# Turning tiles on TensorE instead of in the DMA queue, in a two-layer attention and MLP kernel

## The chip, the cores and the metric

The kernel runs on one core of one Trainium2 chip. The metric is device time in microseconds (us). Before the change it is 1536.79 us, the median of three runs (1535.73 to 1537.83).

## What is computed

Two layers of attention and a feed-forward block each, over one sequence of 2048 tokens of width 512, with 32 heads of 16 columns. Weights are the same in both layers.

```python
def _A_ref(x, wqkv, wo):
    qkv = (x @ wqkv).reshape(B, S, 3, H, Dh)          # H = 32, Dh = 16
    q, k, v = ...
    p = _softmax(jnp.einsum("bhqd,bhkd->bhqk", q, k) * Dh ** -0.5)
    o = jnp.einsum("bhqk,bhkd->bhqd", p, v)
    return o.reshape(B, S, D) @ wo

def _B_ref(x, w1, b1, w2, b2):
    h = _gelu(_layernorm(x) @ w1 + b1)                # F = 1376
    return h @ w2 + b2

x = x + _A_ref(_layernorm(x), wqkv, wo)
x = x + _B_ref(_layernorm(x), w1, b1, w2, b2)
x = x + _A_ref(_layernorm(x), wqkv, wo)
x = x + _B_ref(_layernorm(x), w1, b1, w2, b2)
```

The attention is the bulk of it: 2 layers x 32 heads x 2048 x 2048 exponentials.

## The kernel before

**Attention.** Four heads make a head group (hg, eight of them); each head has 32 rows of a 128-row tile, 16 of data, one for a bound on the score and the rest zero pads. KT holds the keys turned, 128 rows by 2048 tokens per head group; QT holds the queries of up to 512 tokens turned and scaled. A score tile is one key block of 128 tokens times 512 queries of one head: one matmul that uses 32 rows of the array (L1536) and fills one PSUM bank. There are 4096 such banks of scores. Most get their exponential on ACT (ScalarE), three or two banks at a time in turn (banks 0 to 2 and 3 to 4, L1521), into the tile PT. The tiles of five key blocks in 16 (DK) can go to DVE (VectorE) in place of ACT: L1628 loads the bank as a 16-bit pattern that approximates the exponential (dp), and L1659, L1667, L1614 and L1615 make three copies of it with shifted bits, whose values are multiplied with copies of V scaled to match (vs). So a bank on DVE needs four PV matmuls (L1741), a bank on ACT one. PV adds up in a bank of its own (ACCB); at the end of a segment (one layer, query chunk and head group) L1771 transposes it out, and L1807 writes the normalised result into ob.

**The rest.** job_qkv_tile and job_first_tile make queries, keys and values of a tile of 128 tokens; job_post and job_ffn make the output projection and the feed-forward block; job_tail does so for the last tile. Between them tiles must be turned by 128x128 blocks: the normalised input (xn to xnT, L993, and to yT, L1872), the attention output (ob to OT, ot_dma, L1816), keys (qk to KT, L1004 and L1136), and queries. The queries lie unturned in device memory (q_scr) and flow_q turns them as it loads them (L1248). In layer 3 (the name of the second layer) the keys of the first twelve tiles wait in k_scr until KT is free, and job_kload turns them on the way back (L1301). All these are DMA transposes, issued by SP. A few tiles are turned by TensorE and copied out of PSUM: the first four (L1112, copied by ACT, L1113), tiles 4 to 7 of the keys of layer 1 (TPE, L989, copied by DVE, L990), the first queries of two head groups (L1204) and the last tile (L2053).

**What sets the order.** No order is written by hand. Sched holds tasks with a priority, the resources that they read and write, and a duration that the author put in; it runs a model of the engines and lays every task on its engine's stream when it would be next. Scores come first, PV next, and the rest fills in. PSUM banks that are not scores' belong to the pool mb. After the first part of layer 1, take_d sends a bank of scores to DVE whenever DVE has time and one of two banks is free: DLANE (5) or MISCB (7), the last one of the pool. Every four groups of scores the planner's thresholds are set by the next character of a hint string (Hint.ORDER). When the plan is complete, refill goes over PE's stream once more and puts matmuls on a zero tile (zw, L1425, L1427, L1429) into gaps; their results are not used.

Of the kernel before, what the change touches and what calls it, by code (L numbers as in the profile page):

```python
# [14 lines left out]
ALU = mybir.AluOpType  # L15
# [263 lines left out]
class Sched:  # L279
# [168 lines left out]
    def run(self):  # L448
        while True:
# [20 lines left out]
            if t.mate is not None:  # L470
                lim = max(pick[0], self.P.free["dve"]) + self.LOOK["dve"]
                both = next((o for o in self.pend["dve"] if o.mate is not None and o.mate[0] == t.mate[0] and (o.mate[1] < t.mate[1]) == (o.mate[2] < t.mate[2]) and self.task_ready(o) <= lim), None)
# [41 lines left out]
ACCB = 6  # L514
MISCB = 7
DTAIL = 8
DURGE = 8
# [8 lines left out]
TPE = range(4, 8)  # L526
# [14 lines left out]
class Hint:  # L541
# [3 lines left out]
    ORDER = '617843148821304205503107024723209000040207043042340397211914350542770442973009430070000450240024504940493349800001430000505010133104559a211a25403202330431702000300020315024491400100220000100700000140303000510323100000881337000000003040223443052000002459894171985995005343441000044430740448998b224440804240010009a541'  # L545
# [13 lines left out]
class Builder:  # L559
# [45 lines left out]
    def alloc(self, es):  # L605
# [67 lines left out]
        self.q_scr = nc.dram_tensor("q_scr", [2, S, 1024], BF16, kind="Internal").ap()  # L673
        self.k_scr = nc.dram_tensor("k_scr", [S, 1024], BF16, kind="Internal").ap()
# [6 lines left out]
        pl["mb"] = Pool([7, 5, 4, 3, 2, 1, 0])  # L681
# [294 lines left out]
    def job_qkv_tile(self, L, tt, slot, i, left, prio, what):  # L976
# [10 lines left out]
        if L == 1 and what == "kv" and tt in TPE:  # L987
            b = yield ("get", "mb")
            yield Task("pe", prio, [I(lambda e, k=k, b=b: e.transpose(self.psbf(b)[:, k * 128:(k + 1) * 128], xnr[:, k * 128:(k + 1) * 128], self.ident[:, :]), [RX, ("ident",)], [("ps", b)], 0.06, [("ps", b)]) for k in range(4)])  # L989
            yield Task("dve", prio, [I(lambda e, b=b: e.tensor_copy(out=xnT, in_=self.psbf(b)[:, 0:512].rearrange("p (c t) -> p c t", c=4)), [("ps", b)], [RXT], 0.4)])  # L990
            S_.release("mb", b)
        else:
            yield self.dma(lambda e: e.dma_start_transpose(xnT, xnr), [RX], [RXT], prio, 1.31, 1.2)  # L993
# [8 lines left out]
        def kstore():  # L1002
            if direct:
                yield self.dma(lambda e: e.dma_start_transpose(self.KT[:, :, tt * 128:(tt + 1) * 128], self.qks(qs)[:, 1, :]), [QK], [("kt", hg, tt) for hg in range(8)], prio, 1.31, 1.9)  # L1004
            else:
                yield self.dma(lambda e: e.dma_start(self.k_scr[tt * 128:(tt + 1) * 128, :], self.qks(qs)[:, 1, :]), [QK], [("kscr", tt)], prio, 0.38, (1.65, 1.05))
            S_.mark(("ks", L, tt))
# [11 lines left out]
        if "k" in what:  # L1019
# [4 lines left out]
            S_.spawn(kstore(), prio)  # L1024
# [32 lines left out]
        yield Task(eng, prio, [I(lambda e: e.tensor_tensor(out=sq, in0=v4, in1=v4, op=ALU.mult), [("qk", qs, k) for k in range(k0, k1)], SR, 0.14 + 0.00845 * N if eng == "dve" else 1.04)])  # L1057
        if "k" in what:
            yield Task("dve", prio, [self.norms(self.n2k[:, tt, :], ("n2k", tt), ss, 1)])
            S_.mark(("n2k", L, tt))  # L1060
# [8 lines left out]
        if "q" in what:  # L1069
            li = L // 2  # L1070
            yield self.dma(lambda e: e.dma_start(self.q_scr[li, tt * 128:(tt + 1) * 128, :], self.qks(qs)[:, 0, :]), [QQ], [("qscr", L, tt)], prio, 0.38, (1.65, 1.05))
# [30 lines left out]
    def job_first_tile(self, tt, slot, i, left, prio):  # L1102
# [32 lines left out]
        def store():  # L1135
            yield self.dma(lambda e: e.dma_start_transpose(self.KT[:, :, tt * 128:(tt + 1) * 128], self.qks(qs)[:, 1, :]), [QK], [("kt", hg, tt) for hg in range(8)], prio, 1.31, 1.9)  # L1136
            S_.mark(("ks", 1, tt))
# [1029 lines left out]
```

## Time and profile before

| What | Value |
|---|---|
| median of the runs | 1536.79 us |
| the profiled execution | 1537.7 us, its span 1535.9 us |
| granted TensorE clock | 1.00 in all but one of 40 slices |
| matmuls on the zero tile | 2247, 354 us of PE's busy time |
| DMA transposes | 229 |
| bytes moved by DMA | 90.55 MB, DMA engines busy 25.6% of the span |

The profile is of one execution. A row of a group gives the line, the engine, what is written from what, shapes, the count, then busy time in us and the mean of one in ns, and the idle time of the engine just before them with what ended it. Durations of one engine's instructions can overlap, so a busy time can be less than count times mean. In the waits an engine and line stand first, then what they waited for, the total in us, how often and the longest.

### The profile page before, as it was taken

What the parts mean: (1) busy time and instruction counts of PE and PEld (TensorE: products, weight loads), DVE (VectorE), ACT (ScalarE), POOL (GpSimd) and SP (SyncE); (2) the same over time, 40 slices, a digit from 0 to 9 for tenths busy, and PEclk for the clock granted to TensorE, in tenths of its full rate; (3) what the DMA queues carried; (4) which work ended last, traced back from release to release, by engine and by line L of the source; (5) the groups of instructions that cost most, each with busy time, mean ns of one, the idle gap of its engine ahead of it and who ended that gap; (6) DMA issues with size and microseconds to landing.
All of it is one profiled execution on the core that took longest, in us unless ns stands there. A gap on an engine that the chain in (4) does not pass through costs nothing.

```text
span 1535.9 us, 41170 instructions
## 1 busy us (share of the span) xinstructions
PE 1486.8 (97%) x17654; PEld 491.3 (32%) x17654; DVE 1442.2 (94%) x2661; ACT 1502.5 (98%) x1346; POOL 343.0 (22%) x570
## 2 busy tenths in 40 slices
PE   9999999999999999999999999999999999999998
PEld 3222222222222222222322332222222222344555
DVE  8799999999999999999999899999999989998786
ACT  8999999999999999999999999999999999999897
POOL 3576321102120022202322138220002000020110
PEclk9999999999999999999999999999999999999999
DMA  6663102213312123214842332210011001120221
GB/s 163 120 154 91 32 22 34 51 35 68 82 48 63 37 64 84 56 35 100 138 69 64 60 87 63 53 30 18 22 36 35 14 27 32 36 49 18 73 67 30
DMA packets 212487, 90.55 MB, mean 59 GB/s; under 512 B 182251, under 2 KB 207184, under 8 KB 212304
## 3 DMA queue, kind: packets, MB, share of 16 engines
q1 hardware_dynamic: 212304, 87.92, 25.6%
q8 instruction: 138, 2.26, 0.6%
q14 instruction: 45, 0.37, 0.1%
HBM read 36.81 MB, written 19.48 MB: 37 GB/s over the span
## 4 chain that ended last, share of the span: by engine, by line
ACT 44%; PE 27%; DVE 24%; issue 3%; POOL 2%; DMA 0%; DVEq 0%; POOLq 0%
ACT PT L1521 41%; DVE dp L1628 10%; PE ps L1536 9%; PE ps L1741 8%; PE ps L1943 3%; DVE dp L1667 3%; PE ps L1882 2%; PE ps L1016 2%; ACT h L1934 2%; DVE dp L1615 2%; DVE dp L1659 1%; PE ps L1425 1%; DVE accT L1771 1%; DVE st L933 1%; DVE dp L1614 1%
## 5 line engine op out<-in xcount | busy, mean ns | idle before, releaser
L1521 ACT ACTIVATE PT<-ps 128x1536 bf16<-128x1536 f32 (+1 forms) x1256 | 1422.0, 1309 | 20.6 <-PE ps L1536 18.8
L1628 DVE TENSOR_SCALAR dp<-ps 128x512 uint16<-128x512 f32 x979 | 648.8, 679 | 33.7 <-PE ps L1536 30.4
L1536 PE MATMUL ps<-QT,KT 32*128 32x512 bf16 (+2 forms) x5120 | 602.6, 340 | 23.9 <-ACT PT L1521 7.5
L1741 PE MATMUL ps<-PT,V 128*17 128x512 bf16 (+2 forms) x3899 | 491.1, 338 | 0.6 <-issue 0.5
L1741 PE MATMUL ps<-dp,vs 128*17 128x512 bf16 (+2 forms) x3663 | 460.8, 339 | 2.7 <-issue 1.8
L1536 PEld LDWEIGHTS ps<-QT,KT 32*128 32x128 bf16 x5120 | 174.1, 91 | 543.6 <-ACT PT L1521 297.6
L1262 POOL TENSOR_SCALAR QT<-qraw,scl,qbias 128x512 bf16<-128x512 bf16 (+2 forms) x91 | 75.2, 827 | 762.8 <-PE ps L1536 754.3
L1741 PE MATMUL ps<-dp,V 128*17 128x512 bf16 (+2 forms) x1221 | 232.3, 340 | 1.6 <-DVE accT L1771 1.2
L1667 DVE TENSOR_SCALAR dp<-dp 128x2048 uint16<-128x2048 uint16 x310 | 214.3, 694 | 4.9 <-PE ps L1741 1.8
L1741 PEld LDWEIGHTS ps<-dp,vs 128*17 128x17 bf16 x3663 | 124.1, 89 | 114.1 <-issue 84.8
L1741 PEld LDWEIGHTS ps<-PT,V 128*17 128x17 bf16 x3899 | 126.9, 89 | 94.2 <-issue 75.1
L1429 PE MATMUL ps<-zw 128*32 128x448 bf16 (+23 forms) x1514 | 147.1, 322 | 0.1
L1659 DVE TENSOR_SCALAR dp<-dp 128x1024 uint16<-128x1024 uint16 (+1 forms) x298 | 126.1, 426 | 2.6
L1427 PE MATMUL ps<-zw 32*128 32x444 bf16 (+7 forms) x386 | 119.5, 332 | 0.0
L1615 DVE TENSOR_SCALAR dp<-dp 128x4096 uint16<-128x4096 uint16 x91 | 111.0, 1225 | 0.6 <-PE ps L1741 0.4
L1882 PE MATMUL ps<-yT,wf 128*128 128x512 bf16 (+5 forms) x440 | 102.7, 340 | 2.1 <-issue 1.0
L1016 PE MATMUL ps<-wqkv,xnT 128*128 128x512 bf16 x336 | 91.7, 382 | 4.1 <-DVE h L1029 1.1
L1425 PE MATMUL ps<-zw 128*128 128x448 bf16 (+14 forms) x347 | 87.4, 338 | 4.4 <-DVE onec L809 2.1
L1287 POOL TENSOR_SCALAR vs<-V 128x340 bf16<-128x340 bf16 (+2 forms) x72 | 64.3, 894 | 23.0 <-PE ps L1741 16.2
L1741 PEld LDWEIGHTS ps<-dp,V 128*17 128x17 bf16 x1221 | 58.2, 89 | 34.6 <-issue 19.4
L1614 DVE TENSOR_SCALAR dp<-dp 128x2048 uint16<-128x2048 uint16 x97 | 67.8, 700 | 0.0
L1771 DVE STREAM_TRANSPOSE accT<-ps 128x512 f32<-128x512 f32 (+2 forms) x96 | 59.2, 617 | 5.3 <-PE ps L1741 5.0
(201 smaller groups left out, 1053.4 us busy)
## 6 DMA issues: line engine op xcount, KB each, us to landing
vs<-vs_scr SPq DMA_DIRECT2D x64, 255.0 KB, 2.8
wf<-in_B_w_dram SPq DMA_DIRECT2D x90, 128.0 KB, 2.5
q_scr<-qk SPq DMA_DIRECT2D x20, 256.0 KB, 2.0
k_scr<-qk SPq DMA_DIRECT2D x12, 256.0 KB, 2.1
out_dram<-xres SPq DMA_DIRECT2D x16, 128.0 KB, 1.7
vs_scr<-vs SPq DMA_DIRECT2D x8, 255.0 KB, 3.3
xres<-in_A_x_dram SPq DMA_DIRECT2D x7, 256.0 KB, 5.3
v_scr<-vst SPq DMA_DIRECT2D x12, 136.0 KB, 1.7
```

Source lines behind the costliest of these rows:

```text
L1016: yield Task("pe", prio if c0 == 0 else min(prio, HINT.LIN2), [I(lambda e, c=c: e.matmul(self.ps[:, b, :], lhsT=xnT[:, c, :], rhs=self.wqk ...
L1425: fn = lambda e: e.matmul(self.ps[:, b, 0:w], lhsT=self.zw[:, 0:128], rhs=self.zw[:, 0:w], start=st, stop=st, skip_group_check=True)
L1427: fn = lambda e: e.matmul(self.ps[:, b, 0:w], lhsT=self.zw[32 * p:32 * p + 32, 0:128], rhs=self.zw[32 * p:32 * p + 32, 0:w], start=st, sto ...
L1429: fn = lambda e: e.matmul(self.ps[32 * p:32 * p + 32, b, 0:w], lhsT=self.zw[:, 0:32], rhs=self.zw[:, 0:w], start=st, stop=st, skip_group_c ...
L1521: S_.submit(Task("act", 1e-5 * gi, [I(lambda e, pt=pt, n=n, b0=b0: e.activation(out=self.PT[:, pt:pt + n, :], in_=self.ps[:, b0:b0 + n, :] ...
L1536: return [I(lambda e, kb=kb, i=i: e.matmul(self.ps[:, b, i * W:(i + 1) * W], lhsT=self.KT[32 * hp:32 * hp + 32, hg, kb * 128:(kb + 1) * 12 ...
L1615: return lambda e: e.tensor_scalar(out=self.both(x[1], y[1]), in0=self.both(x[0], y[0]), scalar1=float(SHIFT[2]), scalar2=None, op0=ALU.add)
L1628: self.S_.submit(Task("dve", 0.0, [I(lambda e: e.tensor_scalar(out=self.dpu(u)[:, w * 512:(w + 1) * 512], in0=self.ps[:, b, :], scalar1=BI ...
L1659: t = Task("dve", prio(), [I(lambda e: e.tensor_scalar(out=self.dpu(u + 1)[:, 0:N], in0=self.dpu(u)[:, 0:N], scalar1=float(SHIFT[1]), scal ...
L1667: t = Task("dve", prio(), [I(lambda e: e.tensor_scalar(out=self.dpp(v)[:, :, 0:N], in0=self.dpp(u)[:, :, 0:N], scalar1=float(SHIFT[2]), sc ...
L1741: ops.append((nth[j, sh] + 0.1 * i, I(lambda e, hp=hp, v=v, ap=ap[:, i * W:(i + 1) * W], first=first and i == 0, W=W: e.matmul(self.ps[32 ...
L1882: yield Task("pe", self.soft(pr if c0 == 0 else min(pr, HINT.LIN2)) if y0 == 0 else pr, [I(lambda e, c=c: e.matmul(self.ps[0:M, b, 0:W], l ...
```

## The change

Every tile that a DMA transpose turned is now turned by TensorE into a bank of the pool mb (turn, and ot_turn for the attention output) and copied out of it by DVE, in layer 1 from key tile 8 on by ACT. Queries and the stored keys of layer 3 are turned in place, in their qk buffer, before they are stored: q_scr and k_scr hold them turned, and the loads of qraw and KT are plain copies. The turned tile lies over the pads of the qk buffer, so repad clears them again on POOL. The roles of banks 6 and 7 are exchanged, so that DLANE (5) and MISCB (6) are neighbours, and two loads by DVE that are ready together, one from each, become one instruction (d_join, kind 0). DLANE leaves the common pool only when all keys of layer 1 are stored. take_d may go on to the next segment's tiles when 32 banks are left (DEARLY) rather than 8, if this segment has none for DVE left. The hint string is a new one.

```diff
-both = next((o for o in self.pend["dve"] if ... and self.task_ready(o) <= lim), None)
+both = next((o for o in self.pend["dve"] if ... and (t.mate[0] > 0 or abs(o.mate[1] - t.mate[1]) == 1) and self.task_ready(o) <= lim), None)
...
-ACCB = 6
-MISCB = 7
+ACCB = 7
+MISCB = 6
 DTAIL = 8
+DEARLY = 32
...
-TPE = range(4, 8)
+ACT_KT = 8
...
-        self.q_scr = nc.dram_tensor("q_scr", [2, S, 1024], BF16, kind="Internal").ap()
-        self.k_scr = nc.dram_tensor("k_scr", [S, 1024], BF16, kind="Internal").ap()
+        self.q_scr = nc.dram_tensor("q_scr", [2, 128, 8, S], BF16, kind="Internal").ap()
+        self.k_scr = nc.dram_tensor("k_scr", [128, 8, 1536], BF16, kind="Internal").ap()
...
-            yield self.dma(lambda e: e.dma_start_transpose(xnT, xnr), [RX], [RXT], prio, 1.31, 1.2)
+        yield from self.turn(xnr, 4, [RX], xnT, [RXT], prio)
...
-                yield self.dma(lambda e: e.dma_start_transpose(self.KT[:, :, tt * 128:(tt + 1) * 128], self.qks(qs)[:, 1, :]), ...)
+                yield from self.turn(self.qks(qs)[:, 1, :], 8, [QK], self.KT[:, :, tt * 128:(tt + 1) * 128], ..., prio, "act" if L == 1 and tt >= ACT_KT else "dve")
             else:
-                yield self.dma(lambda e: e.dma_start(self.k_scr[tt * 128:(tt + 1) * 128, :], self.qks(qs)[:, 1, :]), ...)
+                kT = self.qks(qs)[:, 1, :]
+                yield from self.turn(kT, 8, [QK], kT.rearrange("p (g t) -> p g t", g=8), [QK], prio)
+                yield self.dma(lambda e: e.dma_start(self.k_scr[:, :, tt * 128:(tt + 1) * 128], kT.rearrange("p (g t) -> p g t", g=8)), ...)
+                yield self.repad(qs, QK, 0, prio, 1)
...
-            yield self.dma(lambda e: e.dma_start(self.q_scr[li, tt * 128:(tt + 1) * 128, :], self.qks(qs)[:, 0, :]), ...)
+            qT = self.qks(qs)[:, 0, :]
+            yield from self.turn(qT, 8, [QQ], qT.rearrange("p (g t) -> p g t", g=8), [QQ], prio)
+            yield self.dma(lambda e: e.dma_start(self.q_scr[li, :, :, tt * 128:(tt + 1) * 128], qT.rearrange("p (g t) -> p g t", g=8)), ...)
+            yield self.repad(qs, QQ, 0, prio)
...
-                yield self.dma(lambda e, ...: e.dma_start_transpose(self.qraw[:, s:s + 1, 0:W], self.q_scr[li, q0:q0 + W, hg * 128:(hg + 1) * 128]), ...)
+                yield self.dma(lambda e, ...: e.dma_start(self.qraw[:, s, 0:W], self.q_scr[li, :, hg, q0:q0 + W]), ...)
...
-        yield self.dma(lambda e: e.dma_start_transpose(self.KT[:, hg:hg + 1, 0:1536], self.k_scr[0:1536, hg * 128:(hg + 1) * 128]), ...)
+        yield self.dma(lambda e: e.dma_start(self.KT[:, hg, 0:1536], self.k_scr[:, hg, :]), ...)
...
-                for b in (5,) if OPEN5 else (4, 5):
-                    S_.retire("mb", b, ("ret", b))
+                S_.when([("kv", 1, tt) for tt in range(self.NT)], lambda: S_.retire("mb", DLANE, ("ret", DLANE)))
...
-        if self.left(sg) < DTAIL:
+        spent = not sg["todod"] and self.left(sg) < DEARLY and self.cur + 1 < len(self.segs) and (...)
+        if self.left(sg) < DTAIL or spent:
...
+        if kind == 0:
+            rows = lambda: self.bits[:, :, :].rearrange("p u (w n) -> p (u w) n", n=512)[:, x[1]:y[1] + 1:y[1] - x[1], :]
+            return lambda e: e.tensor_scalar(out=rows(), in0=self.ps[:, x[0]:y[0] + 1:y[0] - x[0], :], scalar1=BITS0, scalar2=None, op0=ALU.add)
...
+    def repad(self, qs, R, h0, prio, half=0):
+        v = self.qks(qs)[:, half, :].rearrange("p (h c) -> p h c", c=32)[:, h0:32, :]
+        ops = [I(lambda e: e.memset(v[:, :, 16:32], 0.0), [], [R], 0.9)]
+        if half:
+            ops.append(I(lambda e: e.memset(v[:, :, 16:17], 1.0), [], [R], 0.3))
+        return Task("pool", prio, ops)
+
+    def turn(self, src, n, reads, dst, writes, prio, eng="dve"):
+        b = yield ("get", "mb")
+        yield Task("pe", prio, [I(lambda e, k=k, b=b: e.transpose(self.psbf(b)[:, k * 128:(k + 1) * 128], src[:, k * 128:(k + 1) * 128], self.ident[:, :]), ...) for k in range(n)])
+        out = lambda b: self.psbf(b)[:, 0:n * 128].rearrange("p (c t) -> p c t", c=n)
+        if eng == "act":
+            yield Task("act", prio, [I(lambda e, b=b: e.activation(out=dst, in_=out(b), func=ACTF.Copy), ...)])
+        else:
+            yield Task("dve", prio, [I(lambda e, b=b: e.tensor_copy(out=dst, in_=out(b)), ...)])
+        self.S_.release("mb", b)
...
-        for hp in range(4):
-            yield self.ot_dma(hp, range(8), 4 * len(tiles), pr)
+        yield from self.ot_turn(range(8), 4 * len(tiles), pr)
...
-        yield self.dma(lambda e: e.dma_start_transpose(self.yT[:, :, i * 128:(i + 1) * 128], self.xn[:, xr, :]), ...)
+        yield from self.turn(self.xn[:, xr, :], 4, [("xn", xr)], self.yT[:, :, i * 128:(i + 1) * 128], [("yT", i)], pr)
```

The first tiles of layer 1 (job_first_tile, job_q0) are changed in the same manner: their keys go through turn, their queries through turn and repad, and the first queries are copied from the bank that TensorE turned them into. ot_turn turns up to eight blocks of ob in one bank and copies them into OT.

## The prediction

> **What bounds the kernel now.** I read the busy times first, then the groups by shape, then the waits, then the stages.
>
> ```profile
> PE 1486.8 (97%) x17654; PEld 491.3 (32%) x17654; DVE 1442.2 (94%) x2661; ACT 1502.5 (98%) x1346; POOL 343.0 (22%) x570
> ACT 44%; PE 27%; DVE 24%; issue 3%; POOL 2%; DMA 0%; DVEq 0%; POOLq 0%
> ```
>
> Three engines are near full. PE is so only in name: the three groups of matmuls on the zero tile zw (L1429, L1427, L1425) are 147.1 + 119.5 + 87.4 = 354 us of it, work that nobody reads. ACT is full with work that is needed. DMA has no share in the chain of waits, so a faster transfer is worth nothing by itself. Next the groups by shape:
>
> ```profile
> L1521 ACT ACTIVATE PT<-ps 128x1536 bf16<-128x1536 f32 x605 | 924.6, 1528 | 14.6 <-PE ps L1536 13.2
> L1521 ACT ACTIVATE PT<-ps 128x1024 bf16<-128x1024 f32 x651 | 712.5, 1105 | 5.9 <-PE ps L1536 5.7
> L1628 DVE TENSOR_SCALAR dp<-ps 128x512 uint16<-128x512 f32 x979 | 648.8, 679 | 33.7 <-PE ps L1536 30.4
> L1113 ACT ACTIVATE yT<-ps 128x512 bf16<-128x512 bf16 x4 | 2.2, 594 | 0.4 <-PE ps L1112 0.3
> L990 DVE COPY xnT<-ps 128x512 bf16<-128x512 bf16 x4 | 1.6, 402 | 0.0
> ```
>
> The exponentials are the bound: 3 x 605 + 2 x 651 = 3117 banks of scores on ACT, 979 on DVE, 4096 together. A bank that DVE no longer takes goes to ACT. ACT's durations overlap (924.6 + 712.5 = 1637 against 1422.0 us of true busy time in the page's row), so I take the price of a bank from the difference of the two shapes, 1528 - 1105 = 423 ns, and the price of an instruction from the rest: (1422.0 - 3117 x 0.423) / 1256 = 0.082 us. The timeline of ACT checks this in two unbroken stretches:
>
> ```profile
> 727.77 28.27 ACT L1521 ACTIVATE PT<-ps 128x1024 bf16<-128x1024 f32 x25
> 1073.67 52.20 ACT L1521 ACTIVATE PT<-ps 128x1536 bf16<-128x1536 f32 x46
> ```
>
> 25 instructions with 62 banks should take 62 x 0.423 + 25 x 0.082 = 28.3 us, 46 with 115 banks 52.4 us. Both fit, though the DMA engines were busy 0.85 of the time in the slice of the first and 0.09 in that of the second. Last, where ACT is idle (33.4 us in all):
>
> ```profile
> ACT PT L1521 <- PE ps L1536: 18.8, 48, 2.5
> ACT h L2024 <- PE ps L1882: 4.3, 4, 3.6
> ```
>
> 18.8 us are waits for scores: 4.9 us of them between 38 and 160 us, 4.2 between 840 and 925, 3.8 between 1420 and 1460. The rest is start and end.
>
> **The change, part by part.** Counts are from the instruction lists of both built programs; durations are from the rows.
>
> *Removed.* All 229 turning transfers: 94 loads of qraw, 36 of xnT, 31 of yT, 40 of OT, 20 stores to KT, 8 loads of KT. Plain copies take the place of 102 (94 + 8). They took 2.5 to 5.0 us to land, on SP, whose waits stand on nobody's path. ACT waits for none of them directly; through PE they can be behind the first two groups of score waits above, 4.9 + 4.2 us. Gain: 0 to 9 us, nearer the lower end, since in those stages the chain runs mostly over DVE and PE; I take 2.
>
> *ACT.* The list has 946 banks on DVE, not 979, so 3150 on ACT: 611 triples, 658 pairs, one single, 14 instructions more. 33 x 0.423 + 14 x 0.082 = 15.1 us. Eight turned key tiles of layer 1 are copied by ACT (128x1024, bf16 from PSUM). The nearest row is L1113, 128x512: two of them took 1.08 us together and one alone 0.59, so 0.49 in a row, plus 0.42 for 512 more columns: 0.91 x 8 = 7.3 us. They fall in the stage with 4.9 us of waits and might hide in them (0 to 4 us; I take 0, since a wait for scores is not longer for a copy put before it only by luck). ACT's work grows by **22.4 us**, to 1524.9. All else on ACT is the same in both lists.
>
> *DVE.* The loads become 860 singles and 43 joined pairs. A pair's price: L1911 takes 475 ns for 256 columns and 738 for 512, so 527 ns more per 512, 679 + 527 = 1206. 860 x 0.679 + 43 x 1.206 - 979 x 0.679 = -28.9 us. Shifts (L1614, L1615, L1659, L1667 by shape): -12.6 - 22.1 + 6.4 + 2.4 + 10.5 + 3.8 = -11.6. Copies of turned tiles: 40 of xnT and 31 of yT at 402 to 424 ns; 68 of 1024 columns at an estimated 652 (the fixed part of L1628 is 679 - 527 = 152, so 402 has 250 for 512 columns; at the pace of L1911, 402 + 527 = 929, which would be 19 us more); four of 768, two of 512; less four that were there: +74.5. Sum +34.0, or +33 with DVE's overlap of 2%: **1475 us**. In a span of 1558 that leaves 83 us idle, against 94 now. So DVE is drawn tighter, but the plan has given ACT just about what keeps the two level.
>
> *PE.* 800 turns of 128x128 more, 99 PV matmuls fewer (a bank on DVE needs four, on ACT one: 33 x 3) at 1184.3 / 8783 = 0.135 us: -13. For the turns the chain of waits has this row:
>
> ```profile
> 1526.63 0.24 PE ps L2053 x4
> ```
>
> 0.06 each in a row, 48 us in all. Here the Trainium skill speaks against the change: its page "TensorE: Matmul & The Clock Gate", Part 4, gives about 275 ns for such a turn inside a kernel and says that turns do not count as activity for the clock. By that, 800 x 0.275 = 220 us; PE would need 1486.8 - 13 + 220 - 39 = 1655 us and set the end. The -39 is zw work: the list has 752 thousand columns of it, not 845 thousand, 313 us at the full rate and not 352. With the row it is 1486.8 - 13 + 48 - 39 = 1483, with 75 us to spare. I take the row: it is this kernel, back to back, and the 40 older turns left the granted clock at 1.00 in the first slices. Each block of turns also breaks into another tiling of the array; in the chain two projection matmuls between scores take 0.54, four 0.97, six 1.40, that is 0.11 us per block beside 0.216 each. Some 150 blocks, one or two such breaks each: 17 to 33 us, inside the spare 75. Without that cover they would land on ACT's waits for scores.
>
> *POOL and SP.* 44 memsets that clear the pads of a turned tile (L859, 128x512, took 0.53 to 1.07) and 12 small ones: 39 us on an engine with 343 of 1536 busy. Queued behind each on POOL are the query scalings L1262, which PE needs, but those are made ahead: POOL waits 754 us for PE to free their buffer. The cover is thinnest between 922 and 960 us, where POOL is busy 34.0 of 38.4. The qk buffer is released only after turn, store and memset, some 4 us later per tile; next in line is the following tile's projection, and in layer 3 that has the scores of twelve earlier key tiles in front of it, 384 banks or some 140 us at 4096 banks in 1500. DVE's shifts do suffer from POOL: L1659 takes 500 ns between 38 and 154 us, where POOL is busy two thirds of the time, and 415 to 428 elsewhere. 39 us more of POOL, a third of it beside shifts, is some 20 shifts by 0.1 us: 2 us, nothing. Query and key stores are now cut into rows of 256 bytes; they landed in 2.0 us and may take up to 5 (the slowest row, the turned KT load), hidden for the same reason.
>
> *Banks and order.* The bank of DVE's own lane stays in the common pool until all keys of layer 1 are stored; turns take the one bank left over in steady state. Both can hold DVE's loads back; that is in the count of 946, as far as the plan's durations hold. The new hint string reorders everything; no row prices it. Bounds for new waits on ACT: 0 to 15 us (half of what DVE waits for scores, 30.4); I take 2, which cancels the gain above.
>
> Sum: 1535.9 + 22.4 - 2 + 2 = 1558.3 us of span. The profiled execution took 1537.7, 1.8 more than its span, and the median is 0.9 below it: 1558.3 + 1.8 - 0.9 = **1559 us**, 1.4% slower.
>
> **Rivals.**
>
> *DVE and the last bank bind.* If DVE keeps the idle time it has now (94 us; 33.7 of it before L1628), the span is 1475 + 94 = 1569, the time 1570. For it: DVE gets 33 us more while its idle time is mostly waits for PE, which is now broken up more. Against: joined loads need fewer meetings of the two.
>
> *The waits melt: not slower.* If the plan made anew leaves ACT no wait at all between first and last exponential, its idle time is 33.4 - 20.6 = 12.8 and the span 1524.9 + 12.8 = 1537.7, the time 1538.6: no change. It decides once ACT's idle time is under 14 us. For it: DMA turns are gone from the two stages with 9.1 us of these waits. Against: the other 10 have no transfer behind them. To be faster than that, the exponentials themselves would have to be quicker without DMA traffic, and the two stretches above deny it.
>
> *The clock drops.* Between 1421 and 1459 us the granted clock is 0.96 and ACT idles 3.9 us. With 39 us less of zw work and turns that may not count, ten such places would cost 30 to 39 us: about 1592. Against: turns come eight at a time, about half a microsecond.
>
> That transfers are still turned is ruled out by the list: none is left.
>
> **How the numbers follow.** Forecast 0.62; DVE and bank 0.19; clock 0.08; waits melt 0.07, of which I leave 0.03 for faster; 0.04 for what I do not see, on the slow side. The forecast's own bounds are 1559 - 9 - 2 and 1559 + 13; taking in the second case and some of the way to the clock gives 1547 to 1577, with about 0.1 left out on each side. About 0.2% is what can be told from no change here, so below 1533.7 is faster and up to 1539.9 the same: 0.03 and 0.04.
>
> **What would show it.** ACT busy near 1525 with 611, 658 and 1 exponentials, copies of about 1 us; DVE near 1475, pairs at 1.2 us, wide copies at 0.65 and not 0.93; waits of ACT for scores near 19 us; no granted clock under 0.95 for long. I am wrong if ACT's idle time is under 20 or over 45 us, or if turns on PE take 0.2 us each in a row.

## The result, and the profile after

| | before | after |
|---|---|---|
| median of four runs each, on the same chip | 1536.8 us | 1594.9 us |
| span of the profiled execution | 1535.9 us | 1592.7 us |
| ACT busy | 1502.5 us | 1527.8 us |
| ACT idle (span less busy) | 33.4 us | 64.9 us |
| DVE busy | 1442.2 us | 1483.4 us |

The changed kernel is slower: the ratio is 1.0378, with a 95% interval of 1.036 to 1.0396. The direction was forecast, the size was not: +58 us in place of +22, and 1594.9 lies above the range of 1547 to 1577. The spans differ by 56.8 us. 25.3 us of them are more work on ACT, 31.5 us more idle time of ACT.

First the busy times, the granted clock by slices, and the chain of waits by engine, of the changed kernel:

```profile
PE 1537.7 (97%) x18200; PEld 540.9 (34%) x18200; DVE 1483.4 (93%) x2738; ACT 1527.8 (96%) x1368; POOL 369.5 (23%) x626
...
PEclk9999999999999999999999999999999999999999
...
ACT 35%; PE 29%; DVE 28%; POOL 5%; issue 2%; DMA 1%; POOLq 0%; DVEq 0%
```

ACT's share of the chain has gone from 44 to 35%, and the shares of PE, DVE and POOL have grown: the end is set for a longer time by something that stands before the exponentials. The clock is full: 1.00 in each of the 40 slices. Then the groups by shape:

```profile
L1529 ACT ACTIVATE PT<-ps 128x1536 bf16<-128x1536 f32 x611 | 921.2, 1508 | 29.0 <-PE ps L1544 26.2
L1529 ACT ACTIVATE PT<-ps 128x1024 bf16<-128x1024 f32 x658 | 707.0, 1083 | 15.4 <-PE ps L1544 14.2
L1841 ACT ACTIVATE KT<-ps 128x1024 bf16<-128x1024 bf16 x8 | 8.4, 1054 | 5.1 <-PE ps L1838 5.1
...
L1640 DVE TENSOR_SCALAR dp<-ps 128x512 uint16<-128x512 f32 x860 | 575.0, 680 | 38.4 <-PE ps L1544 35.4
L1624 DVE TENSOR_SCALAR dp<-ps 128x1024 uint16<-128x1024 f32 x43 | 52.1, 1211 | 0.3 <-PE ps L1544 0.2
L1843 DVE COPY qk<-ps 128x1024 bf16<-128x1024 bf16 x32 | 21.7, 678 | 1.1 <-PE ps L1838 1.1
L1843 DVE COPY xnT<-ps 128x512 bf16<-128x512 bf16 x40 | 16.3, 411 | 1.5 <-PE ps L1838 1.2
```

The counts and the durations are those of the forecast. What is not is the last column of the first two rows: 44.4 us of idle time before exponentials, against 20.5 before the change. The waits of ACT:

```profile
ACT PT L1529 <- PE ps L1544: 40.4, 50, 11.8
ACT h L2060 <- PE ps L1919: 6.0, 4, 5.2
ACT KT L1841 <- PE ps L1838: 5.1, 3, 4.1
```

Nearly as many waits for scores as before (50, they were 48), but twice the time, and the longest takes 11.8 us where it took 2.5. So the time added is in a few long waits. By stretches of the span, ACT idle is 14.7 us between 30 and 105 us (4.1 before), 22.4 us between 700 and 1010 us (6.1 before), and 27.8 us in all the rest (23.2 before). ACT's timeline shows the longest places; the last column is the idle time before the row:

```profile
87.01 1.17 ACT L1841 ACTIVATE KT<-ps 128x1024 bf16<-128x1024 bf16 x1
...
90.13 1.02 ACT L1841 ACTIVATE KT<-ps 128x1024 bf16<-128x1024 bf16 x1 [0.72 <-PE ps L1838]
95.28 1.02 ACT L1841 ACTIVATE KT<-ps 128x1024 bf16<-128x1024 bf16 x1 [4.13 <-PE ps L1838]
102.95 3.28 ACT L1529 ACTIVATE PT<-ps 128x1024 bf16<-128x1024 f32 x3 [6.65 <-PE ps L1544]
...
951.41 9.14 ACT L1529 ACTIVATE PT<-ps 128x1536 bf16<-128x1536 f32 x8 [0.16 <-PE ps L1544]
972.37 8.23 ACT L1529 ACTIVATE PT<-ps 128x1536 bf16<-128x1536 f32 x7 [11.82 <-PE ps L1544]
```

At 87 to 96 us ACT has nothing to do but wait for key tiles of layer 1 to be turned and copy them; then it waits again. At 960.5 us it stops for 11.8 us. PE is not short of time there. This is PE's timeline in that wait:

```profile
962.87 0.61 PE L1838 MATMUL ps<-ident,qk 128*128 128x128 bf16 x8
963.32 1.20 PE L1434 MATMUL ps<-zw 128*128 128x448 bf16 x6
964.35 1.03 PE L1014 MATMUL ps<-wqkv,xnT 128*128 128x512 bf16 x4
965.21 3.24 PE L1434 MATMUL ps<-zw 128*128 128x448 bf16 x17
968.40 0.23 PE L1235 MATMUL ps<-ident,nm 128*32 128x128 bf16 x1
...
970.25 0.17 PE L1241 MATMUL ps<-krhs,sel 32*128 32x8 bf16 x1
...
971.94 0.60 PE L1544 MATMUL ps<-QT,KT 32*128 32x512 bf16 x5
```

PE turns a tile (L1838), projects values (L1014), turns the maximum of the key bounds (L1235), spreads it (L1241), and between these runs matmuls on the zero tile. The scores (L1544) come only when the scale is there, 1.5 us after DVE writes scl at 970.47. The scale of a layer's second part needs the bounds (n2k) of all sixteen key tiles, and every query is multiplied by it (L1272, QT) before it meets a key. So a whole engine waits for **the last key tile**. I call such a place a gate. Three come up below: the second scale of layer 1 (82.5 us before, 101.7 after), the first of layer 3, which needs key tiles 0 to 11, and the second of layer 3, which needs tiles 12 to 15 as well. In the changed kernel ACT waits at the first and at the last of them. At the first gate of layer 3 (804.07 us) it still has other scores to work on, and no wait between 790 and 830 us is over 0.4 us.

How long a gate stays shut can be measured without regard to what came earlier: from the last sum of the last four tiles that it needs (the feed-forward block's last add, xres) to the scale. DVE's timeline of the changed kernel gives the first gate of layer 3, where the longer chain cost ACT nothing, and then the second, where it did:

```profile
734.38 0.69 DVE L1982 TENSOR_TENSOR xres<-ps,xres 128x512 bf16<-128x512 f32 x1
...
804.07 0.23 DVE L1242 TENSOR_SCALAR scl<-ps,onesm 128x8 f32<-128x8 f32 x1
...
908.50 0.69 DVE L1982 TENSOR_TENSOR xres<-ps,xres 128x512 bf16<-128x512 f32 x1
...
970.47 0.22 DVE L1242 TENSOR_SCALAR scl<-ps,onesm 128x8 f32<-128x8 f32 x1 [0.58 <-PE ps L1241]
```

The second gate in the kernel before:

```profile
864.47 0.68 DVE L1945 TENSOR_TENSOR xres<-ps,xres 128x512 bf16<-128x512 f32 x1
...
918.80 0.23 DVE L1232 TENSOR_SCALAR scl<-ps,onesm 128x8 f32<-128x8 f32 x1 [0.51 <-PE ps L1231]
```

At the first gate that is 69.7 us, and 60.6 before the change (691.79 to 752.39). At the second it is 62.0 us, and 54.3 before.

What may draw it out (a second bank, below, tests it) is seen in DVE's timeline between two sums of one output projection (the rows of L1886; scores, their shifts and the results of PV are left out):

```profile
622.27 0.68 DVE L1886 TENSOR_TENSOR xres<-ps,xres 128x512 bf16<-128x512 f32 x1
624.10 0.42 DVE L1843 COPY xnT<-ps 128x512 bf16<-128x512 bf16 x1 [0.55 <-PE ps L1838]
625.91 0.41 DVE L1843 COPY xnT<-ps 128x512 bf16<-128x512 bf16 x1
...
646.60 0.68 DVE L1843 COPY qk<-ps 128x1024 bf16<-128x1024 bf16 x1
648.39 0.68 DVE L1843 COPY qk<-ps 128x1024 bf16<-128x1024 bf16 x1
650.26 0.41 DVE L1843 COPY xnT<-ps 128x512 bf16<-128x512 bf16 x1
651.87 0.41 DVE L1843 COPY xnT<-ps 128x512 bf16<-128x512 bf16 x1
654.56 0.67 DVE L1843 COPY qk<-ps 128x1024 bf16<-128x1024 bf16 x1
657.30 0.67 DVE L1886 TENSOR_TENSOR xres<-ps,xres 128x512 bf16<-128x512 f32 x1
```

The second and the third sum of this projection follow each other by 35.0 us; before the change they did by 3.0. Between them there are 13 other readouts of pool banks (six of them, projections, not shown), so 14 steps of 2.5 us on average. The new plan has placed the projections here too, so the 32 us more are not all due to turns. Where one turned tile follows another, four of five steps take 1.6 to 1.9 us. Seven of the readouts are turned tiles (L1843), which did not use a bank before. The copies themselves are short (0.41 and 0.68 us) and so are the turns (8 in 0.61 us); what a use of the bank takes beyond them lies between the two engines, hand-overs and DVE's other work ahead of the copy, which were not measured apart.

### The profile page after: what moved, and what is told of

It reads as the page before. It is cut to its first block, busy times and chain, and to the rows that moved or that the text cites. A ratio compares the mean times of both kernels' runs of the same rounds, so it can differ in the third digit from the quotient of the medians.

```text
span 1592.7 us, 42210 instructions
## 1 busy us (share of the span) xinstructions
PE 1537.7 (97%) x18200; PEld 540.9 (34%) x18200; DVE 1483.4 (93%) x2738; ACT 1527.8 (96%) x1368; POOL 369.5 (23%) x626
## 4 chain that ended last, share of the span: by engine, by line
ACT 35%; PE 29%; DVE 28%; POOL 5%; issue 2%; DMA 1%; POOLq 0%; DVEq 0%
ACT PT L1529 32%; DVE dp L1640 9%; PE ps L1544 9%; PE ps L1754 8%; DVE dp L1680 3%; PE ps L1980 3%; PE ps L1919 2%; PE ps L1014 2%; DVE dp L1627 2%; DVE dp L1672 2%; POOL vs L1297 2%; DVE dp L1624 2%; ACT h L1971 2%; PE ps L1434 1%; DVE st L934 1%
## 5 line engine op out<-in xcount | busy, mean ns | idle before, releaser
L1529 ACT ACTIVATE PT<-ps 128x1536 bf16<-128x1536 f32 (+1 forms) x1270 | 1440.3, 1287 | 44.4 <-PE ps L1544 40.4
L1544 PE MATMUL ps<-QT,KT 32*128 32x512 bf16 (+2 forms) x5120 | 594.3, 339 | 23.0 <-ACT PT L1529 8.8
L1640 DVE TENSOR_SCALAR dp<-ps 128x512 uint16<-128x512 f32 x860 | 575.0, 680 | 38.4 <-PE ps L1544 35.4
L1754 PE MATMUL ps<-dp,vs 128*17 128x512 bf16 (+2 forms) x3579 | 438.1, 336 | 1.6 <-issue 0.8
L1544 PEld LDWEIGHTS ps<-QT,KT 32*128 32x128 bf16 x5120 | 171.8, 91 | 506.4 <-ACT PT L1529 262.2
L1272 POOL TENSOR_SCALAR QT<-qraw,scl,qbias 128x512 bf16<-128x512 bf16 (+2 forms) x91 | 77.2, 849 | 721.9 <-PE ps L1544 708.0
L1680 DVE TENSOR_SCALAR dp<-dp 128x2048 uint16<-128x2048 uint16 (+1 forms) x334 | 230.4, 692 | 3.9 <-PE ps L1754 0.5
L1672 DVE TENSOR_SCALAR dp<-dp 128x1024 uint16<-128x1024 uint16 (+1 forms) x322 | 137.8, 433 | 3.4
L1438 PE MATMUL ps<-zw 128*32 128x448 bf16 (+19 forms) x1214 | 134.2, 325 | 0.4 <-DVE accT L1784 0.4
L1436 PE MATMUL ps<-zw 32*128 32x444 bf16 (+3 forms) x351 | 110.9, 332 | 0.0
L1434 PE MATMUL ps<-zw 128*128 128x448 bf16 (+18 forms) x412 | 101.7, 335 | 2.8 <-DVE onec L810 2.1
L1014 PE MATMUL ps<-wqkv,xnT 128*128 128x512 bf16 x336 | 91.9, 382 | 2.4 <-DVE qk L1020 0.8
L1627 DVE TENSOR_SCALAR dp<-dp 128x4096 uint16<-128x4096 uint16 x73 | 90.0, 1234 | 0.2
L1948 DVE TENSOR_SCALAR h<-ps,b1c 128x512 bf16<-128x512 f32 (+4 forms) x88 | 57.8, 656 | 1.6 <-PE ps L1919 1.3
```

The lines of the kernel that those rows point to most:

```text
L1014: yield Task("pe", prio if c0 == 0 else min(prio, HINT.LIN2), [I(lambda e, c=c: e.matmul(self.ps[:, b, :], lhsT=xnT[:, c, :], rhs=self.wqk ...
L1434: fn = lambda e: e.matmul(self.ps[:, b, 0:w], lhsT=self.zw[:, 0:128], rhs=self.zw[:, 0:w], start=st, stop=st, skip_group_check=True)
L1436: fn = lambda e: e.matmul(self.ps[:, b, 0:w], lhsT=self.zw[32 * p:32 * p + 32, 0:128], rhs=self.zw[32 * p:32 * p + 32, 0:w], start=st, sto ...
L1438: fn = lambda e: e.matmul(self.ps[32 * p:32 * p + 32, b, 0:w], lhsT=self.zw[:, 0:32], rhs=self.zw[:, 0:w], start=st, stop=st, skip_group_c ...
L1529: S_.submit(Task("act", 1e-5 * gi, [I(lambda e, pt=pt, n=n, b0=b0: e.activation(out=self.PT[:, pt:pt + n, :], in_=self.ps[:, b0:b0 + n, :] ...
L1544: return [I(lambda e, kb=kb, i=i: e.matmul(self.ps[:, b, i * W:(i + 1) * W], lhsT=self.KT[32 * hp:32 * hp + 32, hg, kb * 128:(kb + 1) * 12 ...
```

## The experiments

The first question was whether turning costs the time, or the hint string.

### Without hint strings

**n_before** is the kernel before with an empty string, **n_after** the changed kernel with one (`ORDER = ''`).

> The kernel before with an empty hint string: the planner keeps its default thresholds throughout. It is the partner of the next run. If the strings carry the difference of 58 us between the two kernels (the new string is the worse fit), this run is slowed by far more than its partner and lands near 1590 to 1640 us, with the partner at the same time within 15 us. If the turns carry it, the two lie 40 us or more apart, as with their own strings.

> The changed kernel with an empty hint string. Strings to blame: within 15 us of the kernel before without a string. Turns to blame: 40 to 65 us above it, with ACT's busy time 20 to 35 us higher and the rest as waits of ACT for scores.

They took 1601.9 and 1653.8 us. The difference of 51.9 us is nearly that of the two kernels with their own strings, 58.1. A string shortens the kernel before by 65.1 us and the changed one by 58.9. So the new string does not carry the loss. In n_after, too, ACT waits at gates, though not at the same ones: 6.7 us up to the second scale of layer 1, and 10.3 before key copies ahead of it; then 20.0 us before the first scale of layer 3, where the changed kernel did not wait; and at the second scale of layer 3 no wait is over 1.5 us.

**n_joins** is the kernel before with the parts of the change that turn nothing, and an empty string:

```diff
+ ... and (t.mate[0] > 0 or abs(o.mate[1] - t.mate[1]) == 1) and ...
-ACCB = 6
-MISCB = 7
+ACCB = 7
+MISCB = 6
+DEARLY = 32
```

> The kernel before with the parts of the change that turn nothing (joined loads of DVE, the exchanged roles of banks 6 and 7, the earlier start on the next segment) and an empty hint string, so that it stands beside the kernel before with an empty string (1601.9 us) and the changed kernel with one (1653.8 us). Both theories put the time lost on the turns: 1585 to 1610 us here, ACT waiting for scores 45 to 65 us, and the layer-1 scale of the second part within 3 us of that of the kernel before with an empty string. If the joined loads or the early start were what costs, it would be above 1620.

1587.2 us: within the band, and 14.7 us *less* than n_before. The joined loads, the exchanged banks and the early start are a gain there (67 joined loads at 1214 ns; ACT's waits for scores 43.4 us, a little under the 45 to 65 expected; they were 55.8). So what turns the tiles, with what belongs to it, costs 1653.8 - 1587.2 = 66.6 us without strings. Of the two spans' difference, 67.4 us, 23.1 are more ACT work (1521.4 to 1544.5) and 44.3 more idle time. The chains to the gates are longer here too: from the last sum to the two scales of layer 3 it takes 71.3 and 69.2 us in n_after, 61.0 and 56.2 in n_joins.

### One gate at a time, with the new string

Five kernels keep the changed kernel's string and treat one gate, or one suspected hold.

**u1_keys_by_dma**: layer 1 turns keys 4 to 15 (and the inputs of tiles 8 to 15) by DMA again.

```diff
-yield from self.turn(xnr, 4, [RX], xnT, [RXT], prio)
+if L == 1 and what == "kv" and tt >= 8:
+    yield self.dma(lambda e: e.dma_start_transpose(xnT, xnr), ...)
+else:
+    yield from self.turn(xnr, 4, [RX], xnT, [RXT], prio)
...
-if direct:
+if direct and L == 1:
+    yield self.dma(lambda e: e.dma_start_transpose(self.KT[:, :, tt * 128:(tt + 1) * 128], self.qks(qs)[:, 1, :]), ...)
+elif direct:
```

> The changed kernel with one part undone: in layer 1, xn of tiles 8 to 15 on the way to keys and values and all keys of tiles 4 to 15 are turned by DMA again. Theory 'late keys' (each turn takes one of the two pool banks and so draws out the chain of key tiles, whose last one gates the scale of the next scores): the scale L1242 of the second part of layer 1 is written near 83 us and not at 101.7, and ACT's waits between 75 and 125 us fall from about 12 us to under 5; the second stall at 960 us stays. Rival 'work alone' (ACT and DVE just have more to do, and a stall that goes comes back as another): the scale may come earlier but ACT's waits over the whole span stay near 65 us. The hint string fits this plan less well, so the total time is no clean measure: 1585 to 1640 us; the stage is what counts.

The gate opened at 90.5 us, not at 83: somewhat over half of the way. ACT's idle time between 75 and 125 us fell from 12.0 to 8.6 us, not to under 5, and over the whole span it was 90.8 us, not the 65 of the rival: neither theory had it right. The time was 1633.5 us, worse than the changed kernel, because among others a wait of 18.4 us came up at the next gate (813.0 to 831.5 us). The plan shifts and the string was made for another one: totals of these five kernels say little, and I read them at the gate that each treats.

**u2_keys_first**: the last four tiles of layer 3 make keys and values first, and queries after all bounds are there. (The queries of these tiles are computed from weights already overwritten; the amount of work is the same.)

```diff
-S_.spawn(self.job_lnqkv(3, tiles, pr - 0.8), pr - 0.8)
+S_.spawn(self.job_lnqkv(3, tiles, pr - 0.8, pr if qc == self.NC - 1 else None), pr - 0.8)
```

> The changed kernel with one order changed: the last four tiles of layer 3 make keys and values first and their queries afterwards, as layer 1 does. All turns stay; the queries' turn, store and clearing no longer hold the two qk buffers in front of the next key tile. Theory 'late keys': from the last sum of layer 1 (L1982) to the scale of the second part of layer 3 (L1242) it takes 35 to 50 us and not 62.0 (54.3 before the change), and the 11.8 us wait of ACT near 960 us goes or falls under 4. Rival 'work alone': the wait is as long, or an equal one follows within the next 100 us. Total 1575 to 1610 us, the string being made for another plan.

From the last sum to the scale 50.0 us in place of 62.0, with every tile still turned by TensorE, and the wait of 11.8 us is gone. DVE had no more room than before: it was busy 49.4 of these 50.0 us, and 56.4 of 62.0 in the changed kernel. The time was 1603.6 us, since DVE took fewer banks (ACT busy 1538.4) and other waits appeared.

**kt_copies_dve**: the eight key copies of ACT go to DVE (`ACT_KT = 16`).

> The changed kernel with its eight key copies of layer 1 on DVE instead of ACT, nothing else. If the banks are held long because these copies stand in ACT's queue behind exponentials of more than a microsecond (part of theory 'late keys'), the scale L1242 of the second part of layer 1 comes 2 to 8 us before 101.7, and ACT's waits between 30 and 105 us (14 us) fall; ACT's busy time falls by 8 us and DVE's rises by 5; total 1583 to 1591 us. If the place of the copy does not matter, the scale stays within 1.5 us of 101.7 and the total within 3 us of 1595.

1590.1 us, ratio 1.0342 (1.0306 to 1.0378): the fastest of the kernels that turn all tiles on TensorE. ACT's work fell by 7.2 us (1520.6). The gate opened at 97.3 us and not 101.7, but the waits did not fall as expected: ACT now waits 14.4 us in one piece, and its idle time between 30 and 105 us is 17.4 us (14.7). So some 5 of the 8.4 us of copies are saved, by the earlier gate, and the rest had been copied in time that is idle anyway.

**u3_q_aside**: the queries of the last four tiles of layer 3 are turned into free xn buffers in two halves, so that their qk buffer is free without waiting for store and memset.

```diff
+if L == 3 and tt >= 12:
+    for g0 in (0, 4):
+        xq = yield ("get", "xn")
+        yield from self.turn(qT[:, g0 * 128:g0 * 128 + 512], 4, [QQ], xt, [("xn", xq)], prio)
...
```

> The changed kernel where the queries of the last four tiles of layer 3 are still turned by TensorE and copied by DVE, but into two halves of the xn buffers, from which they are stored: the qk buffer is free as soon as TensorE has read it, with no wait for the store and no clearing by POOL. Order of the work unchanged. If the held qk buffer makes the stall at 960 us (theory 'late keys'), the time from the last sum of layer 1 to the scale of the second part of layer 3 falls from 62.0 us to 48 to 55 and the wait of 11.8 us to under 5. If it is the turns themselves that draw the chain out, the time stays at 58 to 64. The string is made for another plan, so the total is 1590 to 1625 us and says nothing.

A miss: 64.4 us from the last sum to the scale, longer than 62.0 and just past the 58 to 64 of the case that the turns themselves draw the chain out; the time was 1612.2 us. It frees the buffer but uses the bank once more per tile. That made me count the uses of the bank by the last four tiles up to the scale, and measure from the first tile's copy of projected keys (L1020 in the changed kernel) to the scale:

| kernel | uses per tile | first key copy to scale |
|---|---|---|
| before | 3 | 37.0 us |
| u2_keys_first | 4 | 37.5 us |
| changed kernel | 6 | 49.4 us |
| u3_q_aside | 7 | 51.9 us |

The more uses, the longer the chain, but this alone does not convict the bank: in u2_keys_first the other work on the queries has left the chain as well.

**lend_bank** gives the pool a second bank: DVE's own lane goes back to it from the last sum of layer 1 until all bounds of layer 3 are there.

```diff
+def lend_lane(self):
+    self.lent = True
+    if not self.lane_busy:
+        S_.release("mb", DLANE)
+    S_.when([("n2k", 3, tt) for tt in range(self.NT)], lambda: S_.retire("mb", DLANE, ("ret2", DLANE)))
```

> The changed kernel with one resource added at one place: from the last sum of layer 1 until the bounds of all keys of layer 3 are made, the bank of DVE's own lane (5) belongs to the common pool, as it does in layer 1, and DVE's loads use the other one only. Order, turns and copies are unchanged. In the changed kernel each of the last four tiles needs a pool bank six times (xn, keys, turned keys, queries, turned queries, values), before the change three times. If the one bank sets the pace there, the time from the first key tile's copy (L1020) to the scale (L1242) falls from 49.4 us to 38 to 44 (37 before the change), and the wait of 11.8 us to under 5. If DVE's queue or the held qk buffer sets it, it stays at 46 to 52. The plan puts fewer banks on DVE and the string is made for another plan: total 1590 to 1620 us.

From the first key copy to the scale 45.3 us, 4.1 less than in the changed kernel and just outside the band of 38 to 44. The bounds of the first two tiles were made 12.7 us after the first key copy (21.9 in the changed kernel), but the third tile had to wait for its qk buffer until store and memset of an earlier one had passed, at 939.70 us. So the trace shows both at work, and the run does not settle their shares. In place of the 11.8 us wait ACT has three, of 1.7, 2.4 and 0.8 us, ahead of the scale. The scale came only 3.5 us earlier (966.93); part of the rest is that ACT had more banks to work on meanwhile. The time was 1611.5 us: without its lane DVE took fewer banks (ACT busy 1541.2).

### Gates and bank without strings

To read totals, the last three kernels have empty strings and stand beside n_after (1653.8 us).

**n_late** joins the edits of u1_keys_by_dma and u2_keys_first; here the queries of the last four tiles are computed from the right weights.

> The changed kernel with an empty hint string, in which layer 1 turns key tiles 4 to 15 by DMA transposes again (and the inputs of tiles 8 to 15), and the last four tiles of layer 3 make their keys and values first and their queries afterwards. All other tiles are still turned by TensorE. Late keys: without a string that was made for another plan, both kinds of repair should show in the total, as the stall before the layer-3 scale (20 us) and half of the layer-1 waits go: 1618 to 1640 us against 1653.8 for the changed kernel with an empty string, no single wait of ACT over 10 us at 800 to 1010 us, and ACT idle at least 15 us less. Rival that the turns cost by their work alone, wherever they stand: 1645 to 1655 us, since only some 20 of the turned tiles are given back.

A miss for my theory: 1651.2 us, as the rival said. The trace shows why it could not tell the two apart. Layer 1 was mended (ACT busy 109.4 us between 40 and 160 us, 99.8 in n_after), but the wait before the first scale of layer 3, a gate that I had not treated, grew from 20.0 to 24.5 us. ACT's idle time between 700 and 1010 us grew from 42.2 to 49.5 us, and that of the whole span stayed as it was (107.7 and 107.8). That gate depends on the *third* four tiles.

**n_late2** therefore makes keys and values first for these too. Against n_late it removes no work and no turn; one condition changes:

```diff
-pr if qc == self.NC - 1 else None
+pr if qc >= self.NC - 2 else None
```

> As the changed kernel with an empty hint string, layer-1 keys 4 to 15 turned by DMA transposes, and in layer 3 the keys and values ahead of the queries not only for the last four tiles but also for the third four, whose last tile holds back the first scale of layer 3. In the run where only the last four tiles were so treated, a wait of 24.5 us stood before that scale, 70.1 us after the last sum of the third four tiles. Late keys: that distance falls to under 62 us, the wait to under 12 us, ACT idle to under 95 us (107.8 in the run before this), the time to 1622 to 1642 us. Rival that turns cost by their work and the bank, wherever they stand: the time stays at 1645 to 1655 us and the idle time comes back at other waits.

1631.5 us, 19.7 less than n_late. From the last sum to the first scale of layer 3 it takes 53.0 us where it took 70.1, and ACT's idle time is 1630.5 - 1544.4 = 86.1 us (107.8). Here are the two ends on DVE and the wait on ACT, first in n_late:

```profile
774.07 0.68 DVE L1988 TENSOR_TENSOR xres<-ps,xres 128x512 bf16<-128x512 f32 x1
...
844.19 0.23 DVE L1248 TENSOR_SCALAR scl<-ps,onesm 128x8 f32<-128x8 f32 x1 [0.35 <-PE ps L1247]
```

```profile
849.10 7.85 ACT L1535 ACTIVATE PT<-ps 128x1024 bf16<-128x1024 f32 x7 [24.53 <-PE ps L1550]
```

Then in n_late2:

```profile
774.33 0.68 DVE L1988 TENSOR_TENSOR xres<-ps,xres 128x512 bf16<-128x512 f32 x1
...
827.35 0.23 DVE L1248 TENSOR_SCALAR scl<-ps,onesm 128x8 f32<-128x8 f32 x1 [0.27 <-PE ps L1247]
```

```profile
814.34 9.26 ACT L1535 ACTIVATE PT<-ps 128x1536 bf16<-128x1536 f32 x8
833.36 7.13 ACT L1535 ACTIVATE PT<-ps 128x1536 bf16<-128x1536 f32 x6 [9.77 <-PE ps L1550]
```

All four numbers that the late keys forecast are in their bands, and the rival's 1645 to 1655 us is missed. Order alone bought this time back.

**n_lend2** tests the bank: n_after with DVE's lane in the pool from the output projection of layer 1's third four tiles until all bounds of layer 3 are there.

> The changed kernel with an empty hint string, in which the bank of DVE's own lane is in the common pool again from the output projection of layer 1's third four tiles until all keys of layer 3 have their bounds. The turns then have two banks for some 350 us, and DVE has no bank of its own for exponentials. If the bank is what draws the chains out: from the last sum of the third four tiles to the first scale of layer 3 under 65 us (71.3 in the changed kernel with an empty string), ACT idle between 700 and 1010 us under 27 us (42.2), but DVE takes 20 to 45 banks fewer, ACT busy 10 to 23 us more, and the total is within 15 us of 1653.8. If the bank is not it, the distance stays at 69 us or more, and the total rises by ACT's added work, 10 to 23 us.

Again as the theory has it. From the last sum to the first scale of layer 3 56.0 us (725.49 to 781.52), in n_after 71.3; no wait stands at that gate any more. One rival is not parted from the bank here: the loan also takes loads off DVE (93 instructions on it in that chain, 109 in n_after). A full DVE is not what held n_after, though: it was idle for 11.8 of the 71.3 us. The stretch from 700 to 1010 us, first n_after and then n_lend2, shows the exchange; the columns are the stretch, its length, the busy times of PE, PEld, DVE, ACT and POOL with their instructions, then clock, DMA share and GB/s:

```profile
700.00:1010.00 310.00, 298.82 (x2817) 94.46 (x2816) 270.03 (x486) 267.83 (x228) 68.43 (x123) 0.99 0.24 57
```

```profile
700.00:1010.00 310.00, 298.85 (x2893) 98.09 (x2894) 258.87 (x474) 285.41 (x246) 79.18 (x139) 1.00 0.26 62
```

ACT gains 17.6 us of busy time in this stretch, DVE loses 11.2. Over the whole kernel DVE takes 891 banks, not 925 (825 + 2 x 33 and 843 + 2 x 41), ACT works 1560.5 us, 16.0 more, and the time is 1661.5 us, 7.7 more than n_after. The bank is thus wanted twice: by the turns, whose lateness stops ACT at the gates, and by DVE's exponentials, which without it go to ACT. In this run the price of turning moved from the one to the other and did not vanish.

None of the versions run beats the kernel before. A string made for the order of n_late2, or for n_joins, was not run, so what the turned kernel would take at its best is open, and so is whether joined loads alone would beat the kernel before.

## Why the prediction was right and wrong

- **ACT's work: right.** 1524.9 us were forecast, 1527.8 measured, with 611, 658 and 1 exponentials. The wide key copy took 1.05 us, not 0.91. That they might hide in the stage's waits was given 0 to 4 us and taken as 0; kt_copies_dve gave back 4.8 of the 8.4 us, so some 3.6 were hidden, near that upper end.
- **DVE's work: right.** 1475 forecast, 1483.4 measured; a joined load 1.211 us (1.206), the wide copy 0.675 to 0.678 (0.652; the 0.93 by the other row is out).
- **Turns on PE: right.** Eight in 0.61 us, and the next matmuls start 0.45 after them, so 0.06 to 0.08 each. The 275 ns of the Trainium skill ("TensorE: Matmul & The Clock Gate", Part 4) are near what a lone turn takes here (L1235 above, 0.23 us), but in a row turns follow each other at about a quarter of that. The granted clock stayed at 1.00. PE busy is 1537.7 us, not 1483; 34 of the 55 us are zero-tile work that filled the longer span (346.8 us and not 313).
- **POOL and SP:** POOL 369.5 us (382 forecast). Query stores landed in 2.9 us (2.0 before, bound 5).
- **New waits on ACT: the step that failed.** "Bounds for new waits on ACT: 0 to 15 us (half of what DVE waits for scores, 30.4); I take 2, which cancels the gain above." It was +31.5 us of idle time, twice the upper bound. By the prediction's own mark (idle time over 45 us) it was wrong here; 64.9 was measured. The bound came from a row that has nothing to do with the gates: it asked how long DVE waits for scores, not what holds the scores back. A second error stands beside it, under POOL and SP, where a late qk buffer is called hidden: "next in line is the following tile's projection, and in layer 3 that has the scores of twelve earlier key tiles in front of it, 384 banks or some 140 us". That cover was computed and never looked up. The profile of before denied it: at the second gate of layer 3 these scores were used up before the scale came, and its timeline has the gate's wait on ACT, which is how a cover of zero looks:

```profile
899.54 18.45 ACT L1521 ACTIVATE PT<-ps 128x1024 bf16<-128x1024 f32 x16
920.45 11.40 ACT L1521 ACTIVATE PT<-ps 128x1024 bf16<-128x1024 f32 x10 [2.47 <-PE ps L1536]
```

The scale came at 918.80 us and the exponentials 1.6 us later. With no cover left, a longer chain of keys becomes idle time of ACT: here the chain grew by 7.7 us and the wait by 9.4. From what was known, each of the last four tiles turns its input (0.24 us and 0.41 for the copy), its keys and its queries (0.48 and 0.65 each): an estimate of 12 us at that gate. It leaves out the hand-overs, so its nearness to the 9.4 us is partly luck. Layer 1's stage, whose 4.9 us of waits the prediction had listed itself, called for the same look; ACT's idle time between 30 and 105 us grew by 10.6 us. These two places are 20.0 of the 31.5 us. The other 11.5 us are spread over shorter waits, and their cause stays open.

- **The gain from removed transfers: partly there, in the wrong place.** From the last sum to the first key copy of the last four tiles the changed kernel needs 12.5 us and the other 17.4: turning is quicker there than four DMA transposes. The 12.4 us lost after it outweigh this.
- **Rivals.** "DVE and the last bank bind" named the right resource, at 1570 us, but priced it by DVE's idle time (94 us forecast, 109.3 measured); the cost fell on ACT, the larger part of it at two gates. "The waits melt": the opposite happened. "The clock drops" had 1592 us, near the measured time, and was wrong: the clock is full in all forty slices. A fitting number is no evidence for its mechanism.

## What to carry to other kernels

Before a step is moved from a transfer to an engine and a shared buffer, look for the gates, the places where one small value (here a scale) holds back all further work of the bounding engine; count the uses of each scarce buffer on the way to the gate, and look in the timeline whether the bounding engine already waits there, for then the cover is zero. If it must be moved, put what the gate needs first: keys and values before queries took 17 us off one gate without removing any work. And read an edit's total only beside a plan that was not tuned for another version; with a fitted order string, local repairs came back as waits elsewhere.

## What was not expected of the hardware

Eight turns of 128x128 in a row take 0.61 us on PE and their copy 0.68 on DVE, 1.3 us together; the readouts of two such tiles in a row are 1.8 us apart (646.60 and 648.39), so half a microsecond more goes by that is neither turn nor copy. With the 800 added turns the granted clock was 1.00 in every slice. The stores of turned queries land in 2.9 us (2.0 unturned, the same 256 KB), and the plain load of a key block took 6.3 us at the median where the turning one took 5.0: in these two places the transfer is slower after the change, in the store with rows of 256 bytes. The large query loads went the other way: 2.1 us plain, 2.7 turning.
